# The first 256 tokens of k and q loaded as fp32 by two hardware queues, in an attention and feed-forward kernel

## The chip, the cores and the metric

The kernel runs on one core of a Trainium2 chip. The metric is the device time of one execution in microseconds (us). The kernel before took 326.71 us, the median of three executions (326.46 to 333.23); the execution that the profiler recorded took 326.55 us.

The core has five engines with an instruction queue each, which work in order and wait for each other by semaphores: PE (matrix products and transposes, results in the eight PSUM banks `ps`), DVE and ACT (elementwise work and copies out of PSUM), POOL (masks, copies, and issuing DMAs through a software queue) and SP (issuing DMAs through a hardware queue; ACT can issue through another one). 16 DMA engines carry all of it. PEld is PE's weight loading.

## What is computed

Sliding-window causal attention, its output reordered to tokens x 512, and a gated feed-forward block on it:

```python
scores = scale * np.matmul(q, k.transpose(0, 1, 3, 2))
mask = (rel >= 0) & (rel < window)
scores = np.where(mask, scores, -1000000000.0)
attn = softmax(scores)                      # written out in the reference
x = np.matmul(attn, v).transpose(0, 2, 1, 3).reshape(B * S, H * D)
g, val = x @ w_gate, x @ w_val
out = (g * (1.0 / (1.0 + np.exp(-g))) * val) @ w_out
```

q, k and v are fp32 of shape (8, 8, 576, 64): batch, heads, tokens, head width. The window is 64 tokens. The weights are 512 x 1536, twice, and 1536 x 512. The output is 4608 x 512 in fp32.

## The kernel before

The 4608 tokens are cut into 36 tiles of 128 (`n`) for the attention and 9 chunks of 512 (`c`) for the feed-forward part. Per tile there are scores (`Sb`, lines 479 and 483), the exponential on ACT (L491), the product with v (`AVmm` or `AVs`, L603 for the first tiles), the normalisation on DVE (`AVn`, L619 and L622) and `X`, which turns the result into `xT` (L734 on PE, copied out at L296 or L298). Per chunk, `F` makes two products with the gate and the value weights, for one block `f` of 128 hidden units or two half blocks (L798), tanh on ACT (L804), two DVE operations (L806, L808) into `hT`; `O` multiplies `hT` by the output weights (L829) and stores.

Nothing in the order is left to a scheduler: `build` writes out the order of the opening, the text `EARLY` that of the next stretch, `program` the rest. Each method appends instructions to the engines' queues in the order of the calls, so what stands behind a waiting instruction on an engine waits too. The loads have their own order: `loads` at the start, then the texts `LOADS` and `SHIPS`. Most loads are issued by POOL, which also turns fp32 into bf16 on the way.

The opening in the order of the calls:

- `first_loads` (L745) loads the first 256 tokens of k in fp32 with one transfer on SP (heads 0 to 3 into partitions 0 to 63) and one on ACT (heads 4 to 7 into partitions 64 to 127). A run of 4 tokens of a head, 1 KB, is contiguous in memory. The place is a part of `hT1` that is not yet in use.
- `load2` (L381) loads a pair of tiles of k or q through POOL, here q of pair 0, then k and q of pair 1. Then POOL makes the identity and the masks (L320, L329), loads v of tiles 0 to 3 (L369) and the first weights (`W`, `load_w`, L387): hidden blocks 0-2, 2-4, 4-6, 6-8. `shift` on POOL copies half tiles of v to other partitions (`vs`, L298).
- `warm` (L773) gives PE 48 fillers of 121 columns that multiply zeros. `first_T` (L757) casts k to bf16 on DVE (L298, CAST), turns it by eight 128 x 128 transposes and copies it into `kT`. `T2` (L426) turns a pair by 16 narrower transposes per pair; for q of pair 0 it does it from POOL's load.
- `Sbias` (L459) adds the mask to a bank ahead of the scores. Tiles 0 and 1, then `T2` of pair 1, then the attention of tiles 0 to 3 and the first groups of `F` in 256-token halves.

After the opening, `EARLY` has `k2t q2t` and, between groups of `F`, `k3t`: transposes of later pairs (L423), whose loads are also POOL's.

Of the kernel before, what the change touches and what calls it, by code (L numbers as in the profile page):

```python
# [11 lines left out]
T = B * S  # L12
# [7 lines left out]
BF = dt.bfloat16  # L20
# [146 lines left out]
class _Kernel:  # L167
# [41 lines left out]
    def alloc(self):  # L209
        nc = self.nc  # L210

        def sb(name, n, dtype=BF):
            return nc.alloc_sbuf_tensor(name, [128, n], dtype)

        def ring(name, cnt, n, dtype=BF):
            return [sb("%s%d" % (name, i), n, dtype) for i in range(cnt)]

        self.ident = sb("ident", 128)
        self.mask = sb("mask", 3 * 128)
        self.nmask = sb("nmask", 3 * 128)  # L220
        self.kmask = sb("kmask", 3 * 128)
        self.Wg = sb("Wg", NK * DFF)[:, :].rearrange("p (c f) -> p c f", c=NK)
        self.Wv = sb("Wv", NK * DFF)[:, :].rearrange("p (c f) -> p c f", c=NK)
        self.Wo = sb("Wo", NF * DM)[:, :].rearrange("p (c m) -> p c m", c=NF)
        self.qn = ring("qn", self.NQ, DM)
        self.kn = ring("kn", self.NQ, DM)
        pair = lambda t: t[:, :].rearrange("p (h j d) -> p h j d", h=H, j=2)
        self.qs2 = [pair(t) for t in ring("qs", 2, 2 * DM)]
        self.ks2 = [pair(t) for t in ring("ks", 2, 2 * DM)]
        self.va = [t[:, :].rearrange("p (h d) -> p h d", h=H) for t in ring("va", self.NV, H * 80)]  # L230
        self.vs = [t[:, :].rearrange("p (h d) -> p h d", h=H) for t in ring("vs", 3, H * 80)]
        self.kT = sb("kT", 4 * self.NZ * 128)[:, :].rearrange("p (c t) -> p c t", c=4)
        self.qT = sb("qT", 4 * self.NZ * 128)[:, :].rearrange("p (c t) -> p c t", c=4)
        self.wz = sb("wz", 512)
        self.pt = [t[:, :].rearrange("p (h x) -> p h x", h=H) for t in ring("pt", self.NP, H * 128)]
        self.rc = ring("rc", 2, 8, F32)
        xb = sb("xb", 4 * DM)[:, :].rearrange("p (u m) -> p u m", u=4)
        self.xb = [xb[:, u, :] for u in range(4)]
        self.xb4 = xb.rearrange("p u (h d) -> p u h d", h=H)
        self.rp = sb("rp", 16, F32)  # L240
        xT = ring("xT", self.NX, NK * 512)
        self.xT = [t[:, :].rearrange("p (c t) -> p c t", c=NK) for t in xT]
        self.sig = ring("sig", self.NS, 512)
        self.uu = ring("uu", self.NS, 512)
        hT = ring("hT", self.NH, NF * 512)
        self.hT = [t[:, :].rearrange("p (f t) -> p f t", f=NF) for t in hT]
        self.ost = ring("ost", self.NO, DM, F32)
        f4 = lambda a: a.bitcast(F32).rearrange("p (h j d) -> p h j d", h=4, j=4)
        self.fk = f4(hT[1][:, 0:2048])
        self.fkk = [("hT", 1, f) for f in range(4)]  # L250
        c4 = lambda t: t[:, :].bitcast(BF).rearrange("p (j h d) -> p j h d", j=4, h=4)
        self.ck = c4(self.ost[0])
        self.wup = sb("wup", 1, F32)
        self.psa = nc.alloc_psum_tensor("ps", [128, 4096], F32)
        self.ps = [self.psa[:, 512 * i:512 * i + 512] for i in range(8)]
        self.rot = {"f": ([0, 1, 2, 3], 0), "a": ([4, 5, 6, 7], 0)}
        self.free = None
        self.n_s = 0
        self.late = []
        self.hold = None  # L260
# [478 lines left out]
        self.drop([(bank, bk)])  # L739

    def first_loads(self):
        for gr, eng in ((0, "sp"), (1, "act")):
            d = self.fk[64 * gr:64 * gr + 64].rearrange("p h j d -> p h (j d)")
            a = self.k[0, 4 * gr:4 * gr + 4, 0:256, :].rearrange("h (p j) d -> p h (j d)", j=4)
            self.g.op(eng, lambda e, d=d, a=a: e.dma_start(d, a), reads=self.fkk, writes=[("f", gr)], dma=True)  # L745

    def first_T(self, engs):
        g = self.g
        d = self.ck.rearrange("p j h d -> p h j d")
        self.copy("dve", d, self.fk, [("f", 0), ("f", 1)] + self.fkk, [("ost", 0)])  # L750
        for c in range(2):
            bank, bk = self.bank("a")
            tb = bank[:, 0:256].bitcast(BF).rearrange("p (j t) -> p j t", j=4)

            def pe(e, c=c, tb=tb):
                for j in range(4):
                    r = e.transpose(tb[:, j, :], self.ck[:, j, 2 * c:2 * c + 2, :], self.ident[:, :])  # L757
                return r

            g.op("pe", pe, reads=["ident", ("ost", 0)], writes=[bk])  # L760
            d = self.kT[:, c:4:2, 0:256].rearrange("p g (t j) -> p g t j", j=4)
            a = tb.rearrange("p j (g t) -> p g t j", g=2)
            self.copy(engs[c], d, a, [bk], [("kT", m, c) for m in (0, 1)])

    def warm(self, count, n=512, j=None):
        if j is None:
# [9 lines left out]
        self.g.op("pe", pe, reads=["wz"], writes=[bk])  # L776

    def F(self, c, fs, lo=0, hi=512):
        g = self.g
        nf, n = len(fs), hi - lo  # L780
        w = nf * n
# [9 lines left out]
        for W, wk in ((self.Wg, "Wg"), (self.Wv, "Wv")):  # L791
            bank, bk = self.bank("f")
            bs.append((bank, bk))

            def pe(e, W=W, bank=bank):
                for a, f in enumerate(fs):
                    for kk in range(NK):
                        r = e.matmul(bank[:, a * n:a * n + n], W[:, kk, f * 128:f * 128 + 128], xT[:, kk, lo:hi],  # L798
                                     start=(kk == 0), stop=(kk == NK - 1))
                return r  # L800

            g.op("pe", pe, reads=xk + [(wk, f) for f in fs], writes=[bk], cost=w * 0.0017)
            if wk == "Wg":
                g.op("act", lambda e, G=bank: e.activation(sig[:, 0:w], G[:, 0:w], ACTF.Tanh, scale=0.5), reads=[bk], writes=[("sig", i)])  # L804
        (G, gk), (V, vk) = bs
# [73 lines left out]

    def loads(self):  # L880
        self.first_loads()
        self.load2(0, "q")
        self.load2(1, "k")
        self.load2(1, "q")
        self.init()
        self.init_ident()
        self.init_mask()
        self.init_nmask()
        for n in range(4):
            self.load(n, "v")  # L890
        self.W(0, 2)
        self.load_w("g", 2, 4)
        self.shift(0, 1, "pool")
        self.shift(1, 1, "pool")
        self.load_w("v", 2, 4)
        self.shift(2, 1, "pool")
        self.shift(3, 0, "pool")
        self.W(4, 6)
        self.W(6, 8)

# [181 lines left out]

    def build(self):
        F, S, AV, X, T2, O = self.F, self.S, self.AV, self.X, self.T2, self.O
        self.loads()
        self.banks("a", [4, 5, 6, 7, 0, 1, 2, 3, 4, 5, 0, 1, 2, 3, 4, 5, 6, 7, 0, 1, 2, 3, 4, 5, 6, 7, 6, 7])
        self.warm(48, n=121)
        self.first_T(("dve", "act"))
        s0 = self.Sa(0)
        T2(0, "q", ("act", "dve"))  # L1090
        self.Sbias(s0)
        self.warm(2)
        self.Sb(s0)
        s1 = self.Sa(1, True)
        self.Sb(s1)
        T2(1, "k", ("dve", "act"))
        T2(1, "q", ("dve", "act"))
        self.start()
        s2, s3 = self.Sa(2), self.Sa(3)
        a0, a1, a2, a3 = self.AVa(0), self.AVa(1), self.AVa(2), self.AVa(3)  # L1100
        self.AVs(a0)
        self.shift(1, 0, "dve")
        self.AVn(a0)
        self.shift(2, 0, "dve")
        self.Sbias(s2)
        self.Sb(s2)
        self.AVs(a1)
        self.AVn(a1)
        self.Sbias(s3)
        self.Sb(s3)  # L1110
        X(0, "dve", "a")
        X(1, "dve", "a")
        self.warm(1, j=2)
        self.AVs(a2)
        self.AVn(a2)
        self.AVs(a3)
        self.AVn(a3)
        F(0, (0, 1), 0, 256)
        X(2, "act", "a")
        X(3, "act", "a")  # L1120
        F(0, (2, 3), 0, 256)
        F(0, (0, 1), 256, 512)
        for n in range(4):
            self.did |= {w % n for w in ("s%d", "a%d", "x%d", "Tk%d", "Tq%d")}
        self.main("F0.2-3b")
        self.free = set(range(8))
        self.g.now = dict.fromkeys(self.g.now, max(self.g.now.values()))
        for t in self.program():
            self.pump()
            first = len(self.g.ops)  # L1130
            self.main(t)
            self.at[t] = next((o for o in self.g.ops[first:] if o.eng == "pe"), None)
        self.pump()
        assert not any(self.queues)
        self.g.emit()
# [42 lines left out]
```

## Time and profile before

| | |
|---|---|
| median of three executions | 326.71 us |
| profiled execution | 326.55 us |
| its span, first to last instruction | 324.8 us |
| PE busy | 319.0 us |
| first fillers on PE | 1.30 us |
| cast of k on DVE | 6.27 us |
| first scores (L479) | 9.09 us |
| first group of F (L798) | 16.22 us |
| F0.4, the first 512-token group | 23.66 us |

The span is the time from the first to the last instruction; the 1.75 us between it and the execution's time lie outside what the profile shows. A row of the timeline reads: start, time, engine, line, operation, output <- input, how often, and in brackets the idle time of the engine before it with what ended it. In the DMA view a queue's row has packets, megabytes, and the time its packets took as a share of 16 engines; an issue's row has the size and the time from issue to landing. q0 is POOL's queue, q1 SP's and q10 ACT's.

### The profile page before, as it was taken

The page shows a single profiled execution, that of the slowest core. Times are in us where ns is not written, and L with a number is a line of the kernel's source. Part 1 is how long each engine was busy: PE and PEld are TensorE (multiplying, and loading weights), DVE is VectorE, ACT ScalarE, POOL GpSimd, SP SyncE. Part 2 cuts the span into 40 slices and gives each one's busy share as a digit, 9 for nine tenths or more (in the row PEclk, how much of TensorE's full clock was granted, in tenths as well). Part 3 has the DMA queues.
Part 4 walks back from the last instruction along what each step waited for, and adds up shares of the span by engine and source line. Part 5 has one row for each costly group of instructions (what it writes and reads, how often), then busy time and mean ns, then how long its engine had stood idle before and what let it go on. Part 6 is the DMA issues. An engine that isn't in the chain of part 4 may idle for free.

```text
span 324.8 us, 7949 instructions
## 1 busy us (share of the span) xinstructions
PE 319.0 (98%) x3407; PEld 170.3 (52%) x3407; DVE 204.3 (63%) x354; ACT 135.3 (42%) x243; POOL 110.0 (34%) x138
## 2 busy tenths in 40 slices
PE   6999999999999999999999999999999999999996
PEld 6585578855455445545444454545454544444443
DVE  4778878853557737665757575766656566555520
ACT  2745864545344236343434352525252522322222
POOL 8999990007930702406060607070502000000000
PEclk9999999999999999999999999999999999999999
DMA  9999999999999994999799989999986202100012
GB/s 144 178 190 177 163 167 166 161 142 83 154 147 143 108 168 107 139 153 168 152 158 166 153 115 137 138 123 135 117 113 84 67 32 62 37 34 33 32 64 99
DMA packets 165667, 39.85 MB, mean 123 GB/s; under 512 B 152704, under 2 KB 161152, under 8 KB 165632
## 3 DMA queue, kind: packets, MB, share of 16 engines
q0 software_dynamic: 115152, 18.62, 79.6%
q1 hardware_dynamic: 45024, 11.22, 25.4%
q10 hardware_dynamic: 5456, 9.51, 8.3%
q8 instruction: 27, 0.44, 0.6%
q14 instruction: 8, 0.07, 0.1%
HBM read 37.75 MB, written 9.44 MB: 145 GB/s over the span
## 4 chain that ended last, share of the span: by engine, by line
PE 95%; ACT 1%; POOL 1%; DVE 1%; issue 1%; POOLq 0%
PE ps L798 58%; PE ps L829 28%; PE ps L652 3%; PE ps L516 1%; PE ps L479 1%; ACT pt L491 1%; PE ps L862 1%; PE ps L734 1%; PE ps L483 1%; PE ps L423 1%; PE ps L603 1%; POOL qs L381 1%; PE ps L520 0%; PE ps L459 0%; POOL ks L381 0%
## 5 line engine op out<-in xcount | busy, mean ns | idle before, releaser
L798 PE MATMUL ps<-xT,Wg 128*128 128x512 bf16 (+1 forms) x496 | 111.4, 352 | 0.0
L798 PE MATMUL ps<-xT,Wv 128*128 128x512 bf16 (+1 forms) x496 | 111.2, 352 | 0.0
L806 DVE SCALAR_TENSOR_TENSOR uu<-sig,ps 128x512 bf16<-128x512 bf16 (+1 forms) x109 | 74.0, 679 | 57.6 <-ACT sig L804 57.0
L804 ACT ACTIVATE sig<-ps 128x512 bf16<-128x512 f32 (+1 forms) x109 | 65.0, 597 | 79.5 <-PE ps L798 79.5
L829 PE MATMUL ps<-Wo,hT 128*128 128x512 bf16 x420 | 95.6, 379 | 0.0
L808 DVE SCALAR_TENSOR_TENSOR hT<-uu,ps 128x512 bf16<-128x512 bf16 (+1 forms) x109 | 74.3, 682 | 3.8
L798 PEld LDWEIGHTS ps<-xT,Wv 128*128 128x128 bf16 x496 | 48.5, 98 | 44.9
L369 POOL DMA_DIRECT2D kn<-in_k_dram x31 | 29.3, 949 | 124.0 <-PE ps L829 94.3
L798 PEld LDWEIGHTS ps<-xT,Wg 128*128 128x128 bf16 x496 | 46.7, 98 | 41.4
L829 PEld LDWEIGHTS ps<-Wo,hT 128*128 128x128 bf16 x420 | 40.9, 98 | 48.7
L836 ACT ACTIVATE ost<-ps 128x512 f32<-128x512 f32 x35 | 20.9, 597 | 89.9 <-PE ps L829 83.9
L369 POOL DMA_DIRECT2D va<-in_v_dram x40 | 36.3, 962 | 12.4 <-PE ps L829 12.3
L369 POOL DMA_DIRECT2D qn<-in_q_dram x31 | 29.5, 961 | 0.0
L679 DVE RECIPROCAL rp<-ps 128x14 f32<-128x14 f32 (+1 forms) x28 | 5.7, 203 | 36.3 <-PE ps L652 36.3
L491 ACT ACTIVATE pt<-ps 128x512 bf16<-128x512 f32 x36 | 18.9, 598 | 4.8 <-PE ps L483 4.6
L681 DVE TENSOR_TENSOR xb<-ps,rp 128x896 bf16<-128x896 f32 (+1 forms) x28 | 19.4, 692 | 1.0
L528 ACT ACTIVATE pt<-ps 128x512 bf16<-128x512 f32 x36 | 18.6, 602 | 2.4 <-PE ps L520 2.3
L652 PEld LDWEIGHTS ps<-va,pt 64*64 64x64 bf16 x888 | 10.9, 107 | 6.1 <-issue 5.9
L652 PE MATMUL ps<-va,pt 64*64 64x65 bf16 x888 | 13.5, 194 | 0.1
L537 DVE TENSOR_TENSOR pt<-pt,kmask 128x1024 bf16<-128x1024 bf16 x18 | 12.3, 683 | 0.0
L537 DVE TENSOR_TENSOR pt<-pt,mask 128x1024 bf16<-128x1024 bf16 x14 | 9.4, 685 | 1.1 <-ACT pt L491 1.1
L872 DVE COPY ost<-ps 128x128 f32<-128x128 f32 x1 | 0.3, 291 | 11.8 <-PE ps L862 11.8
(69 smaller groups left out, 149.6 us busy)
## 6 DMA issues: line engine op xcount, KB each, us to landing
out_dram<-ost ACTq DMA_DIRECT2D x35, 256.0 KB, 2.5
va<-in_v_dram POOLq DMA_DIRECT2D x32, 128.0 KB, 6.1
kn<-in_k_dram POOLq DMA_DIRECT2D x25, 128.0 KB, 5.5
qn<-in_q_dram POOLq DMA_DIRECT2D x25, 128.0 KB, 5.6
Wg<-in_moe_w_gate_dram POOLq DMA_DIRECT2D x6, 256.0 KB, 7.1
Wv<-in_moe_w_val_dram POOLq DMA_DIRECT2D x6, 256.0 KB, 7.1
Wo<-in_moe_w_out_dram POOLq DMA_DIRECT2D x2, 768.0 KB, 18.4
qs<-in_q_dram POOLq DMA_DIRECT2D x3, 256.0 KB, 6.5
```

Of the source, the lines that this page charges most:

```text
L369: self.g.op("pool", lambda e, d=d, a=a: e.dma_start(d, a), writes=ks, dma=True, after=self.hold)
L491: g.op("act", lambda e, po=po, p=p: e.activation(po, sv[p], ACTF.Exp, scale=SCALE), reads=[bx[p][1]], writes=[pk[p]])
L528: g.op("act", lambda e, po=po, p=p: e.activation(po, sv[p], ACTF.Exp, scale=SCALE), reads=[bx[p][1]], writes=[pk[p]])
L537: self.g.op("dve", lambda e: e.tensor_tensor(pt, pt, m, ALU.mult), reads=pk + [key], writes=pk)
L652: z = e.matmul(self.psa[64 * c:64 * c + 64, o:o + 65], pt[p][rows, h, 64 * a:64 * a + 64], va[m][rows, h, 0:65], start=first, stop=phase = ...
L681: g.op("dve", lambda e, d=d, num=num, rb=rb: e.tensor_tensor(d, num, rb, ALU.mult), reads=bk + [("rp", k)], writes=xk, cost=(1.0, 0.25)[k])
L798: r = e.matmul(bank[:, a * n:a * n + n], W[:, kk, f * 128:f * 128 + 128], xT[:, kk, lo:hi], start=(kk == 0), stop=(kk == NK - 1))
L804: g.op("act", lambda e, G=bank: e.activation(sig[:, 0:w], G[:, 0:w], ACTF.Tanh, scale=0.5), reads=[bk], writes=[("sig", i)])
L806: g.op("dve", lambda e: e.scalar_tensor_tensor(uu[:, 0:w], sig[:, 0:w], 1.0, G[:, 0:w], ALU.add, ALU.mult), reads=[("sig", i), gk], writes ...
L808: g.op("dve", lambda e: e.scalar_tensor_tensor(out, v3(uu), 0.5, v3(V), ALU.mult, ALU.mult), reads=[("uu", i), vk], writes=[("hT", ih, f) ...
L829: r = e.matmul(OB[:, :], hT[:, f, 128 * u:128 * u + 128], self.Wo[:, f, :], start=(f == 0), stop=(f == NF - 1), skip_group_check=mid is no ...
L836: g.op("act", lambda e: e.activation(ost[:, :], OB[:, :], ACTF.Copy), reads=[ok], writes=[("ost", io)])
```

## The change

The first 256 tokens of q are now loaded like those of k, and both differently. There are four transfers: k on SP and ACT, then q on SP and ACT. SP takes the even heads, ACT the odd heads. A run is 8 tokens, 2 KB; the partition counts 4 heads times 32 runs. POOL no longer loads q of pair 0, and issues q of pair 1 after the masks. Each of k and q is cast by two engines (ACT its odd heads, DVE the even ones), then turned by eight 128 x 128 transposes into two banks and copied out by DVE and ACT. The fillers are 70 of 60 columns. The bias products of tiles 0 and 1 stand between the transposes of k and of q, the transposes of pair 1 around the scores of tile 0. Two DVE shifts go to POOL and one of POOL's to ACT. `F` is also available in steps (`Fs`), and the first groups are interleaved with the attention of tile 3 and with each other.

```diff
     def first_loads(self):
-        for gr, eng in ((0, "sp"), (1, "act")):
-            d = self.fk[64 * gr:64 * gr + 64].rearrange("p h j d -> p h (j d)")
-            a = self.k[0, 4 * gr:4 * gr + 4, 0:256, :].rearrange("h (p j) d -> p h (j d)", j=4)
-            self.g.op(eng, lambda e, d=d, a=a: e.dma_start(d, a), reads=self.fkk, writes=[("f", gr)], dma=True)
+        for x, src in (("k", self.k), ("q", self.q)):
+            for h, eng in ((0, "sp"), (1, "act")):
+                d = self.f32[x][:, h, :, :].rearrange("p j d -> p (j d)")
+                a = src[0, h::2, 0:256, :].rearrange("g (p j) d -> g p (j d)", j=8)
+                self.g.op(eng, lambda e, d=d, a=a: e.dma_start(d, a), reads=self.fkeys[x], writes=[("f", x, h)], dma=True)
+
+    def first_cast(self, x, h, eng):
+        i = "kq".index(x)
+        self.copy(eng, self.c16[x][:, :, h, :], self.f32[x][:, h, :, :], [("f", x, h)] + self.fkeys[x], [("c", x, h), ("ost", i)] if h == 0 else [("c", x, h)])
...
+    def first_T(self, x):
+        st = []
+        for b in range(2):
             bank, bk = self.bank("a")
             tb = bank[:, 0:256].bitcast(BF).rearrange("p (j t) -> p j t", j=4)
...
+                    r = e.transpose(tb[:, j, :], self.c16[x][:, 4 * b + j, :, :], self.ident[:, :])
...
     def loads(self):
         self.first_loads()
-        self.load2(0, "q")
         self.load2(1, "k")
-        self.load2(1, "q")
         self.init()
         self.init_ident()
         self.init_mask()
         self.init_nmask()
+        self.load2(1, "q")
         for n in range(4):
             self.load(n, "v")
         self.W(0, 2)
+        self.shift(0, 1, "pool")
+        self.shift(1, 0, "pool")
         self.load_w("g", 2, 4)
-        self.shift(0, 1, "pool")
         self.shift(1, 1, "pool")
+        self.shift(2, 0, "pool")
+        self.shift(2, 1, "pool")
         self.load_w("v", 2, 4)
-        self.shift(2, 1, "pool")
-        self.shift(3, 0, "pool")
...
-        self.warm(48, n=121)
-        self.first_T(("dve", "act"))
-        s0 = self.Sa(0)
-        T2(0, "q", ("act", "dve"))
-        self.Sbias(s0)
-        self.warm(2)
+        self.warm(70, n=60)
+        self.first_cast("k", 1, "act")
+        self.first_cast("k", 0, "dve")
+        k0 = self.first_T("k")
+        self.first_ev("k", k0, ("dve", "act"))
+        s0, s1 = self.Sa(0, True), self.Sa(1, True)
+        self.first_cast("q", 1, "act")
+        self.first_cast("q", 0, "dve")
+        q0 = self.first_T("q")
+        self.first_ev("q", q0, ("dve", "act"))
+        T2(1, "k", ("dve", "act"))
         self.Sb(s0)
-        s1 = self.Sa(1, True)
+        T2(1, "q", ("dve", "dve"))
         self.Sb(s1)
-        T2(1, "k", ("dve", "act"))
-        T2(1, "q", ("dve", "act"))
         self.start()
-        s2, s3 = self.Sa(2), self.Sa(3)
-        a0, a1, a2, a3 = self.AVa(0), self.AVa(1), self.AVa(2), self.AVa(3)
+        s2 = self.Sa(2, True)
+        a0, a1 = self.AVa(0), self.AVa(1)
...
+        self.shift(3, 0, "act")
+        f0 = self.Fs(0, (0, 1), 0, 256)
+        next(f0)
         self.AVs(a3)
         self.AVn(a3)
-        F(0, (0, 1), 0, 256)
+        next(f0)
         X(2, "act", "a")
+        next(f0, None)
         X(3, "act", "a")
-        F(0, (2, 3), 0, 256)
+        f1 = self.Fs(0, (2, 3), 0, 256)
+        next(f1)
         F(0, (0, 1), 256, 512)
+        next(f1)
+        next(f1, None)
```

Lines 773 and 798 of the profile before are 781 and 810 in the changed kernel; L745 is 746 there and L757 is 760.

More of the change, by code (lines that the diff above doesn't have):

```diff
@@ L247, in alloc @@
         self.ost = ring("ost", self.NO, DM, F32)
[L248 to L252, printed above, removed]
+        f8 = lambda a: a.bitcast(F32).rearrange("p (h j d) -> p h j d", h=2, j=8)
+        self.f32 = {x: f8(hT[1][:, 2048 * i:2048 * i + 2048]) for i, x in enumerate("kq")}
+        self.fkeys = {x: [("hT", 1, 4 * i + f) for f in range(4)] for i, x in enumerate("kq")}
+        c8 = lambda t: t[:, :].bitcast(BF).rearrange("p (j h d) -> p j h d", j=8, h=2)
+        self.c16 = {x: c8(self.ost[i]) for i, x in enumerate("kq")}
         self.wup = sb("wup", 1, F32)
@@ L741, in first_loads @@
     def first_loads(self):
-        for gr, eng in ((0, "sp"), (1, "act")):
-            d = self.fk[64 * gr:64 * gr + 64].rearrange("p h j d -> p h (j d)")
-            a = self.k[0, 4 * gr:4 * gr + 4, 0:256, :].rearrange("h (p j) d -> p h (j d)", j=4)
[L745 to L751, printed above, removed]
+        for x, src in (("k", self.k), ("q", self.q)):
[3 more added lines that the diff above has]
+                self.g.op(eng, lambda e, d=d, a=a: e.dma_start(d, a), reads=self.fkeys[x], writes=[("f", x, h)], dma=True)
@@ L752, in first_T, with pe @@
+    def first_cast(self, x, h, eng):
[4 more added lines that the diff above has]
+        for b in range(2):
             bank, bk = self.bank("a")
             tb = bank[:, 0:256].bitcast(BF).rearrange("p (j t) -> p j t", j=4)
-            def pe(e, c=c, tb=tb):
+            def pe(e, b=b, tb=tb):
                 for j in range(4):
-                    r = e.transpose(tb[:, j, :], self.ck[:, j, 2 * c:2 * c + 2, :], self.ident[:, :])
+                    r = e.transpose(tb[:, j, :], self.c16[x][:, 4 * b + j, :, :], self.ident[:, :])
@@ L758, in pe @@
                 return r
[L760 to L763, printed above, removed]
+            self.g.op("pe", pe, reads=["ident", ("ost", "kq".index(x)), ("c", x, 0), ("c", x, 1)], writes=[bk])
+            st.append((tb.rearrange("p j (g t) -> p g t j", g=4), bk))
+        return st
@@ L765, in warm, with first_ev @@
+    def first_ev(self, x, st, engs):
+        dst = (self.kT if x == "k" else self.qT)[:, :, 0:256].rearrange("p g (t j) -> p g t j", j=8)
+        for b, eng in enumerate(engs):
+            a, bk = st[b]
+            self.copy(eng, dst[:, :, :, 4 * b:4 * b + 4], a, [bk], [(x + "T", m, b) for m in range(2)])
     def warm(self, count, n=512, j=None):
@@ L778, in F, with Fs @@
     def F(self, c, fs, lo=0, hi=512):
+        for _ in self.Fs(c, fs, lo, hi):
+            pass
+    def Fs(self, c, fs, lo, hi):
         g = self.g
@@ L802, in F @@
             g.op("pe", pe, reads=xk + [(wk, f) for f in fs], writes=[bk], cost=w * 0.0017)
+            yield
             if wk == "Wg":
@@ L1085, in build @@
         self.loads()
-        self.banks("a", [4, 5, 6, 7, 0, 1, 2, 3, 4, 5, 0, 1, 2, 3, 4, 5, 6, 7, 0, 1, 2, 3, 4, 5, 6, 7, 6, 7])
-        self.warm(48, n=121)
-        self.first_T(("dve", "act"))
-        s0 = self.Sa(0)
-        T2(0, "q", ("act", "dve"))
-        self.Sbias(s0)
-        self.warm(2)
+        self.banks("a", [6, 7, 0, 1, 2, 3, 4, 5, 6, 7, 4, 5, 6, 7, 0, 1, 2, 3, 4, 5, 6, 7, 2, 3, 0, 1, 2, 3])
+        self.banks("f", [4, 5, 0, 1, 6, 7, 4, 5])
+        self.warm(70, n=60)
[9 more added lines that the diff above has]
+        T2(1, "k", ("dve", "act"))
         self.Sb(s0)
-        s1 = self.Sa(1, True)
+        T2(1, "q", ("dve", "dve"))
         self.Sb(s1)
-        T2(1, "k", ("dve", "act"))
-        T2(1, "q", ("dve", "act"))
         self.start()
-        s2, s3 = self.Sa(2), self.Sa(3)
-        a0, a1, a2, a3 = self.AVa(0), self.AVa(1), self.AVa(2), self.AVa(3)
+        s2 = self.Sa(2, True)
+        a0, a1 = self.AVa(0), self.AVa(1)
         self.AVs(a0)
-        self.shift(1, 0, "dve")
         self.AVn(a0)
-        self.shift(2, 0, "dve")
-        self.Sbias(s2)
         self.Sb(s2)
@@ L1108, in build @@
         self.AVn(a1)
-        self.Sbias(s3)
+        s3 = self.Sa(3, True)
         self.Sb(s3)
+        a2, a3 = self.AVa(2), self.AVa(3)
         X(0, "dve", "a")
         X(1, "dve", "a")
-        self.warm(1, j=2)
         self.AVs(a2)
         self.AVn(a2)
+        self.shift(3, 0, "act")
+        f0 = self.Fs(0, (0, 1), 0, 256)
+        next(f0)
         self.AVs(a3)
         self.AVn(a3)
-        F(0, (0, 1), 0, 256)
+        next(f0)
         X(2, "act", "a")
+        next(f0, None)
         X(3, "act", "a")
-        F(0, (2, 3), 0, 256)
+        f1 = self.Fs(0, (2, 3), 0, 256)
+        next(f1)
         F(0, (0, 1), 256, 512)
+        next(f1)
+        next(f1, None)
         for n in range(4):
```

## The prediction

> **What bounds the kernel now.** I read the busy shares first, then the waits of PE, then the opening in order of time, then the DMA.
>
> ```profile
> PE 319.0 (98%) x3407; PEld 170.3 (52%) x3407; DVE 204.3 (63%) x354; ACT 135.3 (42%) x243; POOL 110.0 (34%) x138
> ...
> DMA  9999999999999994999799989999986202100012
> ```
>
> PE is busy for 98% of the span, and asked for the waits of PE after 16 us the trace names none. So only the time at which the dense stretch begins, and whatever stops it later, can move the end. The DMA row matters as much: the engines are full for the first fifteen slices, so every load that POOL issues there lands when the bytes ahead of it are through.
>
> ```profile
> 0.81 0.74 SPq L745 DMA_DIRECT2D hT<-in_k_dram  x1
> 0.82 0.70 ACTq L745 DMA_DIRECT2D hT<-in_k_dram  x1
> ...
> 6.27 0.67 DVE L298 CAST ost<-hT 128x1024 bf16<-128x1024 f32 x1
> ...
> 7.00 0.62 PE L757 MATMUL ps<-ident,ost 128*128 128x128 bf16 x8 [1.42 <-DVE ost L298]
> ...
> 9.09 0.24 PE L479 MATMUL ps<-qT,kT 64*64 64x128 bf16 x2
> ...
> 16.22 1.05 PE L798 MATMUL ps<-xT,Wg 128*128 128x256 bf16 x8
> ...
> 36.29 0.39 PE L734 MATMUL ps<-ident,xb 128*128 128x128 bf16 x4
> ...
> 36.76 0.46 PEld L423 LDWEIGHTS ps<-ident,ks 128*128 128x128 bf16 x8 [0.26 <-issue]
> ```
>
> The opening: k lands, is cast at 6.27, turned at 7.00, scores start at 9.09, the first group of F at 16.22; from there PE is dense. The last row is the one late stop I use: 0.26 us ahead of the transposes of k's pair 3. That load was issued by POOL at 26.04 and the DMA view of that stretch says:
>
> ```profile
> ks<-in_k_dram POOLq DMA_DIRECT2D x1, 256.0 KB, 10.6
> ```
>
> 26.04 + 10.6 = 36.64: it landed 0.15 us before PE began. So PE and the stream of loads run neck and neck at 36.7 us, and whatever delays that stream delays the end.
>
> **The new loads.** They are 4 transfers of 256 KB, each 128 runs of 2 KB, 512 runs. The old ones were 2 transfers of 256 runs of 1 KB. In the DMA view of the first 20 us:
>
> ```profile
> q1 hardware_dynamic: 272, 0.26, 5.3%
> q10 hardware_dynamic: 272, 0.26, 4.7%
> ```
>
> 272 packets are 256 runs and 16 more, which I read as one closing packet from each of 16 engines. Both sides of those transfers had 64 as outermost count. The new source reads `g (p j) d -> g p (j d)`: 4 head groups outermost, and inside each 32 runs; the destination has 128 partitions. How many engines such a transfer uses no row shows. The ends are 16, as for every load of the trace, and 4, if a transfer is dealt out by whole steps of the outermost loop of both sides: 4 and 128 have no larger common part. I take 4: all loads of the trace have 32 or more outermost on both sides, so their 16 shares fit that reading and the new shape does not fit theirs. I also take the same four engines for SP and ACT.
>
> [...]
>
> **Price of a run.** q10 over the whole span took 8.3% of 16 x 324.8 us for 5,456 packets, mostly 2 KB store rows: 79 ns each. The old 1 KB loads took 4.7% of 16 x 20 us for 272: 55 ns, twice that is 110. I take 85, near the row of the same size; ends 79 and 110. On four engines each carries 128 runs: 128 x 85 = **10.9 us**; on sixteen, 32 runs: 2.7 us.
>
> What those engines no longer carry: old k, 0.52 MB at the best slice's 332 GB/s, 1.6 us; POOL's load of q, 256 KB at the 179 GB/s of 7 to 8 us, 1.5 us; and the room left at 2.0 to 3.0 us, where the DMA share is 0.18 and 0.68, about 0.6 us. Together 3.7. So four engines fall 10.9 - 3.7 = **7.2 us** behind, and each POOL load, which is spread over all sixteen, lands with its slowest share: k's pair 3 at 43.8 in place of 36.64, PE's transposes of it at 44.0 in place of 36.79. Ends: 10.1 - 3.7 = 6.4 and 14.1 - 3.7 = 10.4.
>
> **The way of PE there.** DMA traffic starts in the slice at 2.0 to 2.5; from about 2.3, 10.9 us of runs end at 13.2. If queues take turns on an engine, a POOL packet (1.46 us / 64 per engine = 23 ns) goes between every two runs (170 ns): 13% of the 9 us after POOL's traffic starts, 1.2 us. Landing trails the traffic by 0.8 (the old k of SP landed at 0.81 + 5.2 = 6.0, its GB/s fell off at 5). So q is there at Q = **15.2** (14.0 without turns), k at about 9.5. Behind the casts that wait for them stands everything on ACT and DVE, and behind the transposes everything on PE, by the written order.
>
> From Q to the first group of F, at full pace: cast 0.4 (half of 0.67); transposes and the copy out, 1.5 (7.00 to 8.26 before, with hand-overs); scores of tile 0, 0.4; ACT then copies k's pair 1 and does four exponentials at 0.53, 2.2 past the first hand-over; the scores of tile 2, which wait for DVE's two copies of q's pair 1, keep the next product until +4.7; product 0.4, normalisation 0.9, X 0.3, copy 0.42. Sum 7.0. But between the fillers' end and k's landing PE now has nothing for 4.7 us, and then 2 us of work until Q. The pace after a long pause is shown only at the start:
>
> ```profile
> 1.00:4.40 3.40, 3.10 (x31) 3.11 (x32) 1.00 0.58 149
> ```
>
> These are the fillers (L773) alone, stretch, its length, PE and PEld busy, clock, DMA: 31 in 3.10 us, 100 ns each, where all 48 took 4.29. The 1.4 us pause at 5.6 brought nothing of the kind. Ends: 0, and all of PE's 3 us in this stretch once more. I take the slow pace until scores of tile 2, which adds 1.3: the first F at 15.2 + 8.3 = **23.5** (22.2 at full pace), in place of 16.22.
>
> [...]
>
> From the first F to F0.4 PE does eight groups of 0.87 and X, as before, and now AV3 (0.4): F0.4 at 31.4 in place of 23.66, + 7.7. Before, PE was free for pair 3 at 36.52 (36.29 and four transposes of 56 ns), now at 36.52 + 7.7 = 44.2, the load is there at 43.8. Both routes agree: 44.0 to 44.2 in place of 36.79, **+ 7.3 us**. Behind it nothing is nearer than that wait.
>
> **Edits I cost at nothing.** Fillers: 70 of 60 columns at 50 ns end at 4.8, k is not there. The mask without q's issue ahead of it on POOL: done 1.7 us earlier, no one waits for it now. Casts on two engines, bias matmuls ahead of the scores, copies given to other engines, Fs split: inside the 7.0 above. ACT's second issue (0.7) pushes its table load (1.28) to 3.6, before k. On SP nothing follows the new issue until the transposes at 47 us. On POOL all five shifts (0.6 each) stand ahead of Wv 2-4 and wait for v, which is 7.2 late too: Wg 2-4 is issued at about 19.5 and Wv 2-4 at 22, with 6.5 us to landing; PE wants them at 26.3 and 29.5. Should this cover fail by 1 us, PE waits that 1 us, and most of it comes back at pair 3.
>
> **Sum.** The profiled execution took 326.55 (span 324.8, 1.75 around it), 0.16 under the median. 326.55 + 7.3 = **333.8**.
>
> **Rivals.**
> *Sixteen engines.* The loads are what their title says: 2.7 - 3.7 = -1.0 us on each engine, pair 3 lands at 35.6; PE, with F's first group held only by Wg's landing (issue 9.15 before, 8.3 now, 6.5 to landing less the engines' 1.0), is there in time. 326.55 - 1.0 = **325.6**. It is the case in which the kernel gets faster; it decides at the number of engines alone. For it: every load in the trace uses sixteen. Against: none has so small an outermost count. 0.12.
> *Four engines for SP, four others for ACT.* 64 runs each: 5.4 - 3.7 = +1.7, **328.3**. 0.05.
> *Four engines, and the slow pace lasts into F.* The 3.1 us of slow fillers, laid on F's start, cost 1.6 more, and PE becomes later than the load: 326.55 + 7.4 + 1.6 = **335.6**. 0.08.
> The forecast has 0.75, with 332.5 to 337.0 as its own range.
>
> **Chances.** 2%, 6.5 us (333.1), is about what a measurement of this kernel can tell from no change. Inside the forecast I give 0.78 to more than that: 0.75 x 0.78 + 0.08 = 0.66 slower, 0.01 faster, 0.33 within. The range 331.0 to 338.0 holds the forecast with its ends and the last rival, 0.8; the other two, 0.17, lie under it.
>
> **What would show it.** q1 and q10 in the first stretch with 264 packets (256 runs and 8) if four engines close, 288 if sixteen; PE idle from 4.8 to about 9.5; the cast of q at 15; L810 first at 23.5; L423 at 44. I am wrong if the cast of k starts before 6, or if L810 starts before 17; if both are as I say but the end is not, the stream of loads caught up before 44 us.

## The result, and the profile after

The changed kernel takes 336.68 us (median of six executions, 335.56 to 338.27) against 326.74 us of the kernel before: 1.0308 times as long, 95% interval 1.0295 to 1.0321. Ratios leave out executions that took over 1.5% longer than the fastest of the same kernel, here the 333.23 us of the kernel before. The profiled execution took 336.53 us with a span of 334.5, so 9.7 us of the 10.0 lie in the span. The forecast was 333.8 us, with 331.0 to 338.0 as its range.

The busy shares and the DMA row of the page of the changed kernel:

```profile
PE 320.4 (96%) x3418; PEld 170.5 (51%) x3418; DVE 203.9 (61%) x354; ACT 136.8 (41%) x245; POOL 109.4 (33%) x138
...
DMA  7979999999999999998979796969694421200012
```

PE's work has grown by 1.4 us, the span by 9.7: the time is waiting. The DMA row shows a 7 in the first and the third slice, where the row of before is full. The queues of SP and ACT in the DMA view of the first 20 us, packets, megabytes and share:

```profile
q1 hardware_dynamic: 264, 0.52, 8.3%
q10 hardware_dynamic: 264, 0.52, 8.2%
```

264 is 256 runs and 8 more packets, which I read as two transfers, each closed by four engines. Before, one transfer of 256 runs had 272, 16 more, by the same reading closed by sixteen. The opening in order of time; the brackets tell how long an engine had stood and for what:

```profile
7.66 0.63 ACT L296 ACTIVATE ost<-hT 128x512 bf16<-128x512 f32 x1 [3.59 <-DMA hT<-in_k_dram]
...
11.92 0.43 DVE L298 CAST ost<-hT 128x512 bf16<-128x512 f32 x1 [7.33 <-DMA hT<-in_k_dram]
...
12.41 1.04 PE L760 MATMUL ps<-ident,ost 128*128 128x128 bf16 x8 [7.44 <-DVE ost L298]
...
16.80 0.43 DVE L298 CAST ost<-hT 128x512 bf16<-128x512 f32 x1 [3.06 <-DMA hT<-in_q_dram]
...
17.29 0.62 PE L760 MATMUL ps<-ident,ost 128*128 128x128 bf16 x8 [2.14 <-DVE ost L298]
...
19.27 0.61 POOL L298 COPY vs<-va 64x512 bf16<-64x512 bf16 x1 [9.74 <-DMA va<-in_v_dram]
...
25.07 1.05 PE L810 MATMUL ps<-xT,Wg 128*128 128x256 bf16 x8 [0.25 <-DVE xT L298]
...
46.65 0.61 PE L423 MATMUL ps<-ident,ks 128*128 128x128 bf16 x8 [0.16 <-DMA ks<-in_k_dram]
```

The halves of k land at 7.6 (ACT) and 11.9 (SP), those of q at 14.8 and 16.8. The first group of F starts at 25.07 in place of 16.22, the transposes of pair 3 at 46.65 in place of 36.79: 9.86 us later. Behind that point the two kernels run alike, so the loss is complete there.

One row I had not looked for stands in between. POOL stood for 9.74 us, until v of tile 0 was there, with all further loads queued behind it. Activity by stretch of time (columns: stretch, its length, busy time and count of PE, PEld, DVE, ACT, POOL, clock, DMA share, GB/s), first after, then before:

```profile
9.60:15.00 5.40, 2.59 (x12) 1.29 (x12) 1.12 (x2) 0.80 (x2) 0.00 (x0) 0.50 1.77 193
15.00:20.60 5.60, 3.34 (x90) 2.61 (x90) 2.78 (x5) 2.69 (x6) 1.11 (x2) 0.80 0.52 54
```

```profile
15.00:20.60 5.60, 5.60 (x81) 4.90 (x82) 4.36 (x9) 3.07 (x6) 5.60 (x8) 1.00 1.45 197
```

From 15 to 20.6 the DMA engines moved 54 GB/s; before, 197. The stream of loads was not merely late, it had run dry.

### The profile page after: what moved, and what is told of

It is laid out like the page before. It is cut to its first block, busy times and chain, and to the rows that moved or that the text cites. A ratio compares the mean times of both kernels' runs of the same rounds, so it can differ in the third digit from the quotient of the medians.

```text
span 334.5 us, 7976 instructions
## 1 busy us (share of the span) xinstructions
PE 320.4 (96%) x3418; PEld 170.5 (51%) x3418; DVE 203.9 (61%) x354; ACT 136.8 (41%) x245; POOL 109.4 (33%) x138
## 4 chain that ended last, share of the span: by engine, by line
PE 85%; DMA 8%; POOL 5%; issue 1%; DVE 0%; POOLq 0%
PE ps L810 51%; PE ps L842 27%; DMA va<-in_v_dram 4%; DMA ks<-in_k_dram 3%; PE ps L652 3%; POOL Wg L387 1%; POOL Wv L387 1%; POOL va L369 1%; PE ps L516 1%; PE ps L875 1%; POOL vs L298 1%; PE ps L479 1%; POOL qs L381 1%; POOL ks L381 0%; PE ps L483 0%
## 5 line engine op out<-in xcount | busy, mean ns | idle before, releaser
L652 PEld LDWEIGHTS ps<-va,pt 64*64 64x64 bf16 x888 | 10.8, 107 | 6.1 <-issue 5.9
L760 PE MATMUL ps<-ident,ost 128*128 128x128 bf16 x16 | 1.7, 266 | 9.6 <-DVE ost L298 9.6
```

The costliest lines, as they stand in the source:

```text
L652: z = e.matmul(self.psa[64 * c:64 * c + 64, o:o + 65], pt[p][rows, h, 64 * a:64 * a + 64], va[m][rows, h, 0:65], start=first, stop=phase = ...
```

## The experiments

Eleven kernels were run; ratios are to the kernel before on the same chip. Where a diff names `first_loads`, `first_T`, `loads` or `build`, the code is that of the changed kernel.

### Sixteen engines, all else alike

The source of each first load is read with the 32 runs outermost and the heads inside, so that partition 4p+g holds what 32g+p held; the copies out of the transposes read their columns accordingly.

```diff
-                a = src[0, h::2, 0:256, :].rearrange("g (p j) d -> g p (j d)", j=8)
+                a = src[0, h::2, 0:256, :].rearrange("g (p j) d -> p g (j d)", j=8)
...
-            st.append((tb.rearrange("p j (g t) -> p g t j", g=4), bk))
+            st.append((tb.rearrange("p j (t g) -> p g t j", g=4), bk))
```

> The changed kernel with the loop order of the four first loads turned round: in the source the 32 runs outermost, the 4 heads inside (partition 4p+g in place of 32g+p, and the copy out of the transposes reads the columns in that order). Same bytes, same 2 KB runs, same number of instructions. Theory (the four engines that the outermost count of 4 allows cause the loss): each engine carries 32 runs, about 2.9 us; 288 packets on each hardware queue in the first 20 us; k and q landed by 7.5, v of tile 0 by about 10, POOL waits for v under 1 us, first group of F at 15.5 to 16.5, pair 3 of k lands before 36.5; 325.6 us (324.8 to 326.8). Rival (2 KB runs, the load of POOL in the first us, or the new order of the opening are slow by themselves): first F after 22, time above 333.

Measured: 331.79 us (328.69 to 333.24), ratio 1.0144 (1.0111 to 1.0177). The queues in the first 20 us:

```profile
q1 hardware_dynamic: 288, 0.52, 8.6%
q10 hardware_dynamic: 288, 0.52, 7.6%
```

288 is 256 runs and two times sixteen closing packets. k lands by 4.7, v of tile 0 at 10.80, and POOL stands 1.33 us for it. So the number of engines did what the theory said of the loads. But neither number came true: 4.9 us of the loss went, some 5 stayed. The waits of PE over the whole span, engine, line and what was waited for, total, times, longest:

```profile
PE ps L603 <- issue: 3.1, 1, 3.1
PE ps L760 <- ACT ost L296: 2.9, 2, 2.2
PE ps L781 <- DVE wz L301: 1.3, 1, 1.3
```

PE stood for 3.1 us and waited for nothing that the profile shows ("issue"). In order of time:

```profile
13.21 0.20 PE L603 MATMUL ps<-va,pt 128*64 128x65 bf16 x1
...
16.54 0.19 PE L603 MATMUL ps<-vs,pt 128*64 128x65 bf16 x1 [3.13 <-issue]
...
18.94 1.89 PE L810 MATMUL ps<-xT,Wg 128*128 128x256 bf16 x8
```

The stop is in the middle of one group of products. The first group of F behind it takes 1.89 us where 1.05 is usual, and the granted clock is 0.50 from 19 to 21 us, so PE also ran at half pace for a while. Pair 3 of k was transposed at 41.25 without a wait: here PE was late, not the load. A queue that I had not watched, the page's row "q8 instruction" (27 packets, 0.44 MB, so 16 KB each), had a packet at 14.24 that took 0.95 us. PE went on 1.35 us after its end.

### POOL's order in the changed kernel

Four engines again; all weights are issued ahead of the shifts that wait for v.

```diff
         self.W(0, 2)
+        self.W(2, 4)
+        self.W(4, 6)
+        self.W(6, 8)
         self.shift(0, 1, "pool")
         self.shift(1, 0, "pool")
-        self.load_w("g", 2, 4)
         self.shift(1, 1, "pool")
...
-        self.load_w("v", 2, 4)
-        self.W(4, 6)
-        self.W(6, 8)
```

> The changed kernel with POOL's order of issues changed: all weights up to block 8 are issued ahead of the five shifts that wait for v. Theory (pair 3 of k is late because POOL stands still for 10 us and issues it at 35.4, and PE by itself is as late): the load of pair 3 is issued at about 31 and lands at 43.5 to 45; the first F stays at 25.1, PE reaches the transposes of pair 3 at 46.35 and no longer waits; gain 0.3 us, 336.2 (335.7 to 336.7). Rival (the stream of loads alone sets the end): 334.0 to 334.8.

Measured: 338.85 us (337.89 to 339.13), ratio 1.0364 (1.0347 to 1.0381): slower than the changed kernel, which neither theory had. The load did as expected: issued at 31.38 in place of 35.42, there at 44.93 in place of 46.51, and PE no longer waits for it. But PE came later:

```profile
24.98 0.19 PE L603 MATMUL ps<-vs,pt 128*64 128x65 bf16 x1 [1.35 <-issue]
27.39 1.05 PE L810 MATMUL ps<-xT,Wg 128*128 128x256 bf16 x8 [0.26 <-DVE xT L298]
...
48.64 0.61 PE L423 MATMUL ps<-ident,ks 128*128 128x128 bf16 x8
```

Now that the DMA engines are busier at 20 to 24 us (158 GB/s, against 93 in the changed kernel), the stop by "issue" is here too, at the same place of the program: in both traces 449 recorded instructions of PE (weight loads, products and eight of its sequencer) precede it. The 16 KB packet started at 22.59; in the changed kernel itself, whose engines were little used then, it came at 20.01, PE reached that place at 22.66, and nobody stood. So the dry stretch of the stream seems to have hidden a second cost.

### PE kept busy in the changed kernel

Three runs have more fillers: 200 and 28 in the first, the same with POOL's order of the last section in the second, 287 and 85 in the third.

```diff
-        self.warm(70, n=60)
+        self.warm(200, n=60)
...
         s0, s1 = self.Sa(0, True), self.Sa(1, True)
+        self.warm(28, n=60)
```

> The changed kernel with 200 fillers in place of 70 and 28 more between the bias products and the transposes of q, so that PE's pauses stay under 2.5 us. Theory: the matmuls from the transposes of k to the second product with v run at the full pace, the first F starts at 23.7 in place of 25.07, and PE then waits 1.5 us in all for loads, most of it at pair 3 of k, which still starts at 46.65: time unchanged, 336.5 (336.0 to 337.0). Rival (PE alone sets the end): 335.1. Rival (the slow pace is not from the pause): first F at 25.1.

Measured: 337.19 us (336.37 to 337.63), first F at 25.47. Inconclusive: the 200 fillers took 7.68 us, 38 ns each, and ended at 9.0, PE then stood 3.4 us for k, and the first product with v still ran at the slow pace (0.65 us in place of 0.44).

> Both edits: weights ahead of the shifts, and the fillers. Theory: first F at 23.7, pair 3 of k landed by 45, its transposes at 45.0; 335.0 (334.4 to 335.6), more than the two edits gain alone. Rival (only one of PE and the stream matters): as much as the better of the two alone.

Measured: 336.84 us (336.58 to 337.17), first F at 26.04, the load of pair 3 issued at 31.53 and there before PE, which transposed it at 47.29. Not the 335.0 expected; the fillers left a pause of 4.3 us.

> The changed kernel (four engines) with 287 fillers first and 85 between the bias products and the transposes of q, which leaves PE no pause above 1 us (in the run with 200 and 28 a filler took only 37 ns, so that the pauses were 3.6 and 1.6 us). Theory: all matmuls from the transposes of k on run at the full pace, first F at 23.4 to 24.0 in place of 25.07; the transposes of pair 3 still start when their load is there, at 46.6, after a wait of 1 to 1.7 us: time unchanged, 336.6 (336.0 to 337.2). Rival (PE alone sets the end): 335.1 to 335.5. Rival (the slow pace is not from the pauses): first F at 25.

Measured: 336.93 us (336.42 to 337.23), ratio 1.0310 (1.0295 to 1.0324). This one reached its aim:

```profile
10.06 1.92 PE L781 MATMUL ps<-wz 128*128 128x60 bf16 x64 [1.19 <-issue]
...
16.53 1.08 PE L781 MATMUL ps<-wz 128*128 128x60 bf16 x33 [1.52 <-issue]
17.45 0.61 PE L760 MATMUL ps<-ident,ost 128*128 128x128 bf16 x8
...
23.88 1.05 PE L810 MATMUL ps<-xT,Wg 128*128 128x256 bf16 x8 [0.20 <-DVE xT L298]
...
46.38 0.61 PE L423 MATMUL ps<-ident,ks 128*128 128x128 bf16 x8 [1.08 <-DMA ks<-in_k_dram]
```

From the transposes of q to the first F it takes 6.43 us; in the changed kernel 7.78. So the slow pace cost 1.35 us, and it comes from the pauses: the granted clock is 1.00 from 5 to 48 us here, where the changed kernel has 0.50 from 19.13 to 22.55. Pair 3 now waits 1.08 us for its load, and the time is that of the changed kernel: the load of pair 3 sets the end as well as PE does. The two stops by "issue" are among the fillers here, behind 449 and 705 recorded instructions, 256 apart.

### Is the stop code?

If the two stops are 256 apart because PE's code comes in pieces of 256 instructions by DMA, the stop has to move through the program when the number of instructions ahead changes, and to go when the piece is asked for while the engines are free. Both edits are made to the kernel with sixteen engines.

```diff
-        self.warm(70, n=60)
+        self.warm(25, n=160)
```

> The same with 25 fillers of 160 columns: 90 instructions fewer ahead. Theory (code): the pause comes 90 instructions later in the program, about the third product with v or the first group of F, again behind 449 recorded loads and products, and lasts 1 to 2.5 us. Rival (the product with v): it stays in the second product with v.

Measured: 329.56 us (one execution). The stop is in the third product with v, again behind 449:

```profile
14.90 0.20 PE L603 MATMUL ps<-vs,pt 128*64 128x65 bf16 x1
16.70 0.26 PE L603 MATMUL ps<-va,pt 128*64 128x65 bf16 x1 [1.60 <-issue]
```

```diff
-        self.warm(70, n=60)
+        self.warm(100, n=40)
```

> The kernel with the loop order turned round (sixteen engines) and 100 fillers of 40 columns in place of 70 of 60. That puts 60 more instructions (a weight load and a product for each filler) ahead of the transposes of k. In the sixteen-engine kernel PE stood still for 3.1 us at 13.4, in the middle of the second product with v, without a wait; a 16 KB packet on the queue of instructions started at 14.24, and PE went on 1.4 us after its end. PE's 449 first loads and products stand ahead of that place, in this kernel and in the one with the weights ahead of the shifts. Theory (PE ran out of code, its next 16 KB is asked for 256 instructions before and came 4.4 us later because the DMA engines are full): the packet is asked for at 5.7, ahead of most POOL traffic, and lands before PE gets there: no pause above 0.5 us after the transposes of q, granted clock 1.00 from 15 on, first F at 15.3 to 15.8; pair 3 of k waits 0.5 to 1 us for its load, which POOL issues at 27.0; 327.7 us (326.6 to 328.6). Rival (the pause belongs to the product with v, its inputs or its banks): it stays there, 331 to 332.

Measured: 328.74 us (328.37 to 329.30), ratio 1.0064 (1.0051 to 1.0077). The packet starts at 7.58 and PE has no such stop (its longest wait by "issue" is 0.2 us); the first F is at 15.45 and takes 1.05. The edit took away 3 us (2.6 by the ratios). It changes the number and the width of the fillers and nothing else, and they end at 4.8 in both kernels, so it is the number of instructions that did it. The time is just above the range I gave, since the load of pair 3 was later than I had taken it:

```profile
39.25 0.60 PE L423 MATMUL ps<-ident,ks 128*128 128x128 bf16 x8 [1.78 <-DMA ks<-in_k_dram]
```

The packets fit pieces of about 256 recorded instructions: 0.44 MB in 27 packets of 16 KB for 2 x 3418 loads and products, 26 packets where a run has 2 x 3356, 29 where it has 2 x 3703, which is 253, 258 and 255 to a packet, and stops 256 apart. That PE stands because it waits for such a packet is inferred from this. How long a piece is under way when the engines are full, the page does not say; here the packet started 4.4 us after the 193rd recorded instruction (256 ahead of the stop) in the first kernel with sixteen engines, 2.1 us after it in the changed kernel, whose engines were little used. That the piece is asked for at that instruction is inferred. That full engines are what delays it is not shown either: the two kernels of the next section that differ in the loop order alone have 2.6 us (sixteen engines) and 1.4 us (four), though the engines moved less in the first, 173 GB/s against 205 from 4.4 to 5.9. What is shown is that the stop moves and goes with the number of instructions.

### The last 2 us, and the four engines by themselves

In the kernel of the last run POOL stood 1.75 us for v of tile 0 with nothing issued. The kernel before has Wg 2-4 ahead of its first shift; so has this one:

```diff
+        self.load_w("g", 2, 4)
         self.shift(0, 1, "pool")
         self.shift(1, 0, "pool")
-        self.load_w("g", 2, 4)
+        self.load_w("v", 2, 4)
         self.shift(1, 1, "pool")
         self.shift(2, 0, "pool")
         self.shift(2, 1, "pool")
-        self.load_w("v", 2, 4)
```

> The kernel with 16 engines and 100 fillers of 40 columns, and on POOL the issue of Wg 2-4 ahead of the first two shifts, Wv 2-4 ahead of the other three, as much as the kernel before had. Theory: POOL no longer stands 1.3 us for v of tile 0 with nothing issued, pair 3 of k is issued 0.7 us earlier and lands at 36.9; 327.0 us (326.0 to 327.9), the same as the kernel before. Rival (the load does not set the end): as e16_code.

Measured: 326.50 us (326.18 to 329.33), ratio 1.0003 (0.9986 to 1.0021). The rest of the change, with these three repairs, costs nothing and brings nothing.

```profile
15.53 1.05 PE L810 MATMUL ps<-xT,Wg 128*128 128x256 bf16 x8 [0.20 <-DVE xT L298]
...
36.96 0.61 PE L423 MATMUL ps<-ident,ks 128*128 128x128 bf16 x8
```

F starts 0.7 us earlier than before, but has the product of tile 3 inside, and pair 3 is transposed at 36.96 against 36.79. Its load landed at 36.82.

Then the loop order alone was put back in this kernel (the two lines of the first experiment).

> The kernel with 100 fillers and Wg 2-4 ahead of the first shifts (326.5 with sixteen engines), with only the loop order of the four first loads put back: 4 heads outermost, four engines. Theory (the number of engines is the cause of the loss): q lands at 16.8 again, POOL stands 8 us for v of tile 0, the first F at 25, pair 3 of k issued at 34.6 and there at 45.6, PE reaches it at 46.3 by itself; 336.3 (335.6 to 337.2), 9.8 above the same kernel with sixteen engines. Rival (the engines cost half, the rest was code): 331 to 332.

Measured: 337.34 us (336.88 to 339.36), ratio 1.0336 (1.0305 to 1.0367), 10.8 us above the same kernel with sixteen engines (10.9 by the ratios; the two ran on different chips).

```profile
19.78 0.61 POOL L298 COPY vs<-va 64x512 bf16<-64x512 bf16 x1 [9.50 <-DMA va<-in_v_dram]
...
26.49 1.05 PE L810 MATMUL ps<-xT,Wg 128*128 128x256 bf16 x8 [0.20 <-DVE xT L298]
...
47.75 0.61 PE L423 MATMUL ps<-ident,ks 128*128 128x128 bf16 x8
```

v of tile 0 lands at 19.72, and pair 3 is transposed without a wait for its load, which landed at 45.97. That is 1 us more than expected: the transposes of q and the work behind them ran at the slow pace to 23.2. In this kernel the loop order of four loads accounts for the whole loss. In the changed kernel as it stood, the other order alone gave back 4.9 us of 10, because the stop after 449 instructions (3.13 us) and POOL's order then showed.

### Two tries for a faster kernel

```diff
-            for h, eng in ((0, "sp"), (1, "act")):
+            for h, eng in ((0, "sp"), (1, "act" if x == "k" else "sp")):
...
-        k2.2 q2.2 Wg8-10 Wv8-10 v4 v5 Wg10-12 Wv10-12 k3.2 q3.2 v6 v7 ...
+        k2.2 q2.2 Wg8-10 Wv8-10 v4 v5 k3.2 Wg10-12 Wv10-12 q3.2 v6 v7 ...
```

> The kernel with sixteen engines, 100 fillers and Wg 2-4 ahead of the first shifts, and two more edits: both halves of q on SP (the half on ACT landed 3 us after that of SP), and the load of k's pair 3 ahead of Wg and Wv 10-12. Theory (both PE and the load of pair 3 set the end at 36.8, PE by the late q): q there at 6.8, scores of tile 0 at 8.8, first F at 15.2 (bounded by Wg, 14.96), pair 3 of k there at 34.5, its transposes at 36.4, no wait; 326.0 (325.5 to 326.5). Rival (Wg and Wv of the first blocks set PE's pace up to there): 326.4 to 326.7.

Measured: 327.69 us (325.94 to 333.97), ratio 1.0021 (0.9990 to 1.0052). The second half of q landed at 8.0 on SP as it had at 8.3 on ACT, so the queue is not what delays it; perhaps it is that this transfer shares the engines with POOL's loads, whose first packet is at 4.6. No run tests that. Pair 3 was there at 34.9, and PE reached it at 36.66, 0.3 us earlier. Five of the twelve times are at 325.9 to 326.6, the others go up to 334; what makes them differ I did not settle.

The second edit alone, in the kernel before:

> The kernel before, with the load of k's pair 3 ahead of Wg and Wv 10-12 alone. It lands at 34 in place of 36.66; PE's stop of 0.26 us at 36.5 goes, Wv 10-12 is there at 36.7, before it is wanted. Theory: 0.2 to 0.3 us faster, 326.4. Rival (the loads behind are then late): no gain or a loss to 0.5.

Measured: 326.42 us (326.13 to 327.86), ratio 0.9996 (0.9983 to 1.0009). The load landed at 34.4 and the stop at pair 3 went, but another of 0.3 us for v came up in the opening, and pair 3 was transposed at 36.83 as before. No kernel was found that beats the kernel before beyond its uncertainty.

## Why the prediction was right, and where its terms were off

The time lay in the range, the sign and the cause were right, and the size was 7.3 us forecast against 10.0. The difference, step by step:

**Four engines, the same for SP and ACT: right.** Besides the 264 packets, the marks of the semaphores say so. The first load of k by SP has one mark at 2.16 and four at 11.69 to 11.90, where the old one had sixteen. POOL's load of k's pair 1, spread over all sixteen, had twelve shares in by 6.65 and the last four at 16.70 to 16.96. The kernel with the loop order put back shows that this is the cause of the loss. What the single mark at 2.16 stands for was not shown. The 4 came from taking the largest common part of the outermost counts, which was my estimate; the runs show it for these loads only, 4 heads outermost with four engines and 32 runs outermost with sixteen.

**85 ns a run: the sum came out, its parts are not shown. A POOL packet between every two runs: it fits the landings.** Together they make 85 + 23/2 = 97 ns per run. The DMA view from 4.8 to 14.0, while both queues ran:

```profile
q0 software_dynamic: 5123, 1.04, 144.1%
q1 hardware_dynamic: 188, 0.38, 12.7%
q10 hardware_dynamic: 182, 0.36, 11.3%
```

These are 370 hardware packets, 12 of them closing ones: 4 x 9.2 us / 370 = 99 ns. The turns fit the landings: one POOL packet for two of the hardware queues' until 14.0, then one for each of SP's 75, makes 370/8 + 75/4 = 65 POOL packets on an engine by 16.5; POOL's load of k's pair 1 has 64 on each, and its four late shares landed at 16.70 to 16.96. The price is another matter. 12.7% and 11.3% of sixteen engines are 96% of four, so a hardware packet took 95 ns, not 85, with next to nothing between two; packets overlap in this view (q0 alone has 144.1%), so where POOL's turns lie does not show. That 97 met 99 is in part luck. The 79 ns at the low end, too, is a mean with 592 closing packets of 4 bytes in it; the 2 KB packets of q10 in the kernel before took 91 ns each.

The step that failed is that both queues start together and end together. ACT's first packet came at 2.26, SP's at 4.80 (2.31 and 3.26 in the kernel before); why, no row shows. And one queue alone takes 124 ns per packet (82 from 2.26 to 4.80), 133 at the end (75 from 14.0 to 16.5). So k was complete at 11.9 in place of 9.5, and PE stood until 12.4; q was there at 16.8, not at 15.2: **+1.6 us**.

**From q to the first F, 8.3 us: 8.29 measured** (16.78 to 25.07). The terms named for the 7.0 us at full pace add up to 6.7; the 0.51 us from q's landing to its transposes and the 6.43 of the run with more fillers make 6.9. How long a pause brings the slow pace no row of before shows; in the changed kernel the granted clock was 0.50 from 10 to 15 us, where PE had stood from 4.8 to 12.4, and again from 19.13 to 22.55. The 1.3 us for it came to 1.35, but not where it was put: the transposes of q ran at full pace (0.62 us at 17.29), and the slow stretch went from the transposes of q's pair 1 (0.95 us at 18.97) to the scores of tile 2 (until 22.6).

**From the first F to F0.4, 7.9 us: 8.41** (33.48 less 25.07), **+0.5**. I had counted the groups' own 0.87 us, X and 0.4 for the product of tile 3; the gap between the first two groups alone, 25.94 to 26.43, is 0.49 for that product, and the rest is two longer steps of PE, 0.32 and 0.35 us ahead of the instructions at 27.52 and 29.10, where 0.11 is usual. What PE waited for there was not traced.

**The stream of loads: right in effect, wrong in its mechanism.** The prediction had "each POOL load lands with its slowest share", 7.2 us behind on full engines. The loads that were already issued did so (v of tile 0 at 19.21 in place of 10.59). But the later ones waited for POOL, and the engines ran dry. The failed step is the sentence on the five shifts among the edits costed at nothing: it compared Wg and Wv 2-4 with the time at which PE wants them, and left out every load behind them in POOL's queue, pair 3 of k among them. Its own figure for Wv 2-4, 22 us, and the 13.5 us from there to pair 3 in the kernel before (12.57 to 26.04) would have put the issue at 35.5; it came at 35.42. That is 9.38 us later than before, and the load landed 9.85 later, not 7.2. With the weights issued ahead of the shifts it landed 1.58 us earlier. As PE was late by itself, this added only the last **0.3 us**, PE's wait at pair 3.

The remaining **0.3 us** lies outside the span (336.53 - 334.5 = 2.03, against 1.75). Sum: 7.3 + 1.6 + 0.5 + 0.3 + 0.3 = 10.0.

**The rivals.** *Sixteen engines* would have given 331.8, not 325.6: the stop after 449 instructions and POOL's order stood behind it, and no part of the 1.0 us that I gave it as a gain shows. v of tile 0 lands at 10.8 to 11.2 with sixteen engines, against 10.59 in the kernel before and 11.66 in the kernel before with pair 3 moved, whose loads up to there are the same. So no gain shows in the loads, but one trace does not tell a difference of 1 us here; what does is the time, which with all three repairs is that of the kernel before. *Two sets of four engines* falls with POOL's shares: four of them are late, not eight. *The slow pace lasting into F* did not happen: the first group took 1.05.

## What to carry to other kernels

Look at the loop order of the source of a hardware-queue load before anything else: 4 heads outermost and 32 runs inside used four engines, the other order of the same loops sixteen, and here that was 10.8 us of 337. When an instruction on the engine that issues loads has to wait longer, follow every load behind it to its own deadline, not only the next. And when instructions are added to or taken from PE in a stretch of short instructions, count what stands ahead: here PE stood behind 449 and behind 705 recorded instructions, 256 apart, for 1.19 to 3.13 us, and 30 more and narrower fillers ahead took the 3.13 us away. That it waited for its code, in the 16 KB packets, is inferred.

## What the runs showed that I had not expected

- PE stood without a wait that the profile shows for 3.13, 1.60, 1.35, 1.19 and 1.52 us in four kernels, always behind 449 or 705 recorded instructions of PE. That it stood for code is inferred. The kernel before comes near it: its packet started at 12.0, PE went on 2.3 to 2.5 us after the start of the packet in the kernels that stood, and it had the first instruction behind the 449 at 14.26.
- In the changed kernel one hardware queue alone on its four engines took 124 to 133 ns per packet (2 KB runs, and the few that close a transfer), two together 99 ns.
- A pause of 1.6 us was enough for the half pace in one kernel: after the stop at 14.9 the products ran at half pace from 16.8 to 20 (the first F again 1.89 us, the granted clock 0.50 from 17 to 20), with PE busy for 1.40 of the 3 us from 14 to 17. A single pause of 1.7 us in the best kernel, at 7.4 to 9.1, had no such effect (the transposes of q behind it took 0.61 us, the granted clock was 1.00), so it is not the pause alone that decides.
- The profile's clock does not always show it: in the kernel with the loop order put back the eight transposes of q took 1.03 us in place of 0.62, and the clock of those stretches is given as 1.00.
